# A gated mix of a long convolution and a routed feed-forward layer: down weights in a second set of buffers, wider transpositions, small steps on other engines, a new written order

## The chip, the core and the metric

The kernel runs on one core of a Trainium2 chip. The core has TensorE (PE), VectorE (DVE), ScalarE (ACT), GpSimd (POOL) and SyncE (SP), which here issues nearly all transfers. The metric is device time in microseconds (us) of one execution, lower is better.

## What is computed

Inputs are 2048 tokens of 512 channels, all fp32. Cut to its core:

```python
def reference(q, k, v, shift_k, ssm_k, ssm_D, w_r, w_gate, w_up, w_down, gate_w):
    g = sigmoid((q * gate_w).sum(-1, keepdims=True))
    kv = short_conv(k, shift_k) * v             # 4 causal taps per channel
    y = long_conv(kv, ssm_k) + kv * ssm_D       # 2048 taps per channel, by FFT
    a = q * y
    r = q @ w_r                                 # router: a score per token
    idx = argsort(-r)[:2]                       # the two best tokens
    x = q[idx]
    f = (silu(x @ w_gate) * (x @ w_up)) @ w_down * sigmoid(r[idx])
    b = q with f added at rows idx
    return g * a + (1 - g) * b
```

## The kernel before

The 512 channels are four groups c of 128. For each group the long convolution is a Fourier transform in two factors, 64 x 32. The step names are those of the written order:

- *taps c.x* (L166 to L179): a quarter of the short convolution. ACT multiplies by the first tap (L170). The other three are on DVE, each one instruction (L174), where TAPS has "D", or are an ACT multiply into one of two `tap` buffers (L177) and a POOL add (L179) where it has "A". Quarters 0 and 1 read one loaded kT tile, 2 and 3 the next.
- *T* (L190, L194): PE transposes two quarters; DVE multiplies by v, giving kv.
- *D* (L143): POOL adds the skip weights `drow` into rows 0 and 64 of a loaded filter tile hN. *A* (L161) transforms the filter, *C* (L206) transforms kv; an exchange by 32x32 transpositions on DVE (L152) follows each.
- *S u* (L219, L224, L231), u = 0 to 7: second factor on PE, then ACT copies half of the product, and DVE makes the complex products y. After each pair of u, two sums of 512 columns join them (L239), by SUMS on POOL ("G"), on DVE ("V"), or not at all ("E"): then PE takes more products in I.
- *I* (L259, L267, L269): inverse second factor and eviction, by EVICT on ACT or DVE. *X* (L276): DVE transposes f in place, after both I. *J* (L295 to L314): inverse first factor, gate and residual on ACT (L309) and POOL (L312), store. For the last group gate and residual are prepared by *Q* (L284, L287) and finished on DVE and POOL (L301, L304).

*G* is one step of the routed layer: the router's products on q (L341), two searches for the largest score (L328 to L365), an indirect DMA that gathers two rows (L375), gate and up products (L409), down products (L426), and an update (L434, L436). *Z0* (L439) adds the update to the stored output by an indirect DMA, which comes behind all stores.

*L* steps load: Lh (hN, 2 buffers), Lk (kT, 2), Lv (v, 3), Lq (q, 4), Lw (the tiles of q transposed, then gate, up and down weights, all in `wff`, 2 buffers), L0 to L11 constants. All loads and stores stand in one queue on SP; one that waits for its buffer holds those behind it.

The text ORDER names the steps. Each name advances its generator to its next `yield`, and each engine runs its instructions in that order. Products go to PSUM tiles `p2` with three buffers, so PE runs at most three of them ahead of what reads them.

## Time and profile before

| | us |
|---|---|
| median of 3 runs (range) | 167.28 (166.28 to 170.13) |
| the profiled execution | 168.12 |
| its span | 166.3 |
| PE busy | 133.7 (80%) |
| DVE busy | 125.6 (76%) |
| POOL busy | 108.7 (65%) |
| ACT busy | 99.8 (60%) |
| DMA | 39.73 MB, mean 239 GB/s |

A span runs from the first to the last instruction. A group's row gives the line, the engine, what is written and read, the count, the busy time, the mean of one in ns, and the idle time of the engine before them with what ended it. One PE product is two records in the trace, so counts of PE rows are double those of the order.

### The profile page before, as it was taken

To read this page: it belongs to the slowest core of one execution; us is meant where nothing else is said; L and a number is where in the kernel's file an instruction comes from. 1 tells how busy PE (TensorE), PEld (TensorE's weight loads), DVE (VectorE), ACT (ScalarE), POOL (GpSimd) and SP (SyncE) were. 2 spreads that over 40 slices of the span, in tenths; PEclk is the share of its full clock that TensorE was granted. 3 is DMA by queue.
4 is the path that set the end of the run, shared out by engine and by line. 5 is a ranking of instruction groups with operands and counts; after the bars stand their busy time and mean duration, and the time that the engine had idled before them with its cause. 6 is when DMAs were issued, how large, how long until landed. Compare 5 with 4: busy or idle time off the path is not lost.

```text
span 166.3 us, 4904 instructions
## 1 busy us (share of the span) xinstructions
PE 133.7 (80%) x2036; PEld 61.3 (37%) x2036; DVE 125.6 (76%) x140; ACT 99.8 (60%) x188; POOL 108.7 (65%) x103
## 2 busy tenths in 40 slices
...
GB/s 142 265 380 312 341 341 362 302 309 222 342 417 307 8 123 353 130 73 279 195 325 324 165 200 236 240 180 286 233 221 230 128 310 147 318 262 116 234 196 1
DMA packets 16377, 39.73 MB, mean 239 GB/s; under 512 B 2264, under 2 KB 2786, under 8 KB 16228
## 3 DMA queue, kind: packets, MB, share of 16 engines
...
q14 instruction: 5, 0.04, 0.1%
HBM read 35.22 MB, written 4.20 MB: 237 GB/s over the span
## 4 chain that ended last, share of the span: by engine, by line
PE 58%; DMA 16%; DVE 14%; issue 4%; SPq 2%; POOL 2%; ACT 2%; POOLq 1%; DVEq 0%
PE p L219 11%; PE p L259 11%; PE p L206 9%; PE p L161 7%; PE ps L295 5%; DMA wff<-in_wd_dram 5%; PE pf L409 4%; DMA wrg<-in_wrg_dram 4%; DVE f L276 4%; DMA pe<-in_qrow_dram,ti 3%; PE pf L341 3%; DMA kT<-in_kT_dram 2%; PE p L295 2%; DVE e L152 2%; DVE y L231 2%
## 5 line engine op out<-in xcount | busy, mean ns | idle before, releaser
L179 POOL TENSOR_TENSOR acc<-acc,tap 128x512 f32<-128x512 f32 x36 | 46.0, 1287 | 4.7 <-ACT tap L177 2.0
L231 DVE TENSOR_TENSOR y<-p,g 128x1024 f32<-128x1024 f32 x32 | 37.6, 1213 | 9.1 <-ACT g L224 5.6
L152 DVE STREAM_TRANSPOSE e<-p 128x1024 f32<-128x1024 f32 x32 | 38.3, 1234 | 5.3 <-PE p L206 3.6
L239 POOL TENSOR_TENSOR y<-y 128x512 f32<-128x512 f32 x30 | 38.2, 1292 | 4.4 <-DVE y L231 4.3
L219 PE MATMUL p<-e,w 64*32 64x256 f32 x1024 | 34.6, 387 | 2.0 <-DVE y L231 1.6
L177 ACT ACTIVATE tap<-kT,shk 128x512 f32<-128x512 f32 x36 | 25.7, 718 | 8.7 <-POOL acc L179 8.7
L224 ACT ACTIVATE g<-p 128x512 f32<-128x512 f32 x32 | 19.2, 603 | 13.1 <-PE p L219 11.4
L309 ACT ACTIVATE acc<-ps,omg,gcol 128x128 f32<-128x128 f32 x48 | 18.1, 458 | 12.4 <-PE ps L295 12.0
L312 POOL TENSOR_TENSOR qN<-acc,qN 128x512 f32<-128x512 f32 x12 | 15.4, 1290 | 12.4 <-ACT acc L309 12.4
L219 PEld LDWEIGHTS p<-e,w 64*32 64x32 f32 x1024 | 16.9, 106 | 17.8 <-ACT f L267 3.7
L276 DVE STREAM_TRANSPOSE f<-f 128x1024 f32<-128x1024 f32 x16 | 19.1, 1226 | 0.8 <-ACT f L267 0.7
L267 ACT ACTIVATE f<-p 128x1024 f32<-128x1024 f32 x15 | 16.0, 1097 | 5.3 <-PE p L259 5.3
L259 PE MATMUL p<-y,w 32*64 32x512 f32 x272 | 19.1, 600 | 0.0
L161 PE MATMUL p<-hN,w 64*128 64x512 f32 x64 | 18.1, 656 | 0.9 <-DVE e L152 0.6
L170 ACT ACTIVATE acc<-kT,shk 128x512 f32<-128x512 f32 x16 | 11.3, 715 | 11.0 <-DMA kT<-in_kT_dram 10.4
L206 PE MATMUL p<-kv,w 64*128 64x512 f32 x64 | 17.2, 646 | 0.7 <-DVE e L152 0.5
L143 POOL TENSOR_TENSOR hN<-hN,drow 1x32 f32<-1x32 f32 x16 | 4.3, 266 | 19.5 <-DMA drow<-in_drow_dram 12.1
L190 PE MATMUL p<-ident,acc 64*128 64x64 f32 x128 | 6.5, 240 | 11.8 <-DVE acc L174 9.6
L295 PE MATMUL ps<-f,vv 128*64 128x128 f32 x192 | 13.2, 277 | 0.1
L174 DVE SCALAR_TENSOR_TENSOR acc<-kT,shk,acc 128x512 f32<-128x512 f32 x12 | 8.7, 749 | 6.1 <-ACT acc L170 5.9
L295 PEld LDWEIGHTS ps<-f,vv 128*64 128x64 f32 x192 | 10.3, 134 | 7.2 <-issue 3.7
L194 DVE TENSOR_TENSOR kv<-p,vN 128x512 f32<-128x512 f32 x16 | 10.6, 690 | 2.9 <-PE p L190 1.5
...
## 6 DMA issues: line engine op xcount, KB each, us to landing
...
```

The lines of the kernel that those rows point to most:

```text
L152: nc.vector.transpose(ee[c][:, i, b * 16:(b + 1) * 16].rearrange("p d k e -> p d e k"), p)
L161: nc.tensor.matmul(p[:, j], w1[r], hs.get(t)[r, 16 * (b % 2):16 * (b % 2) + 16], start=True, stop=True)
L177: nc.scalar.activation(s, w[j], AF.Copy, scale=shk[:, c, j:j + 1])
L179: nc.gpsimd.tensor_add(acc, acc, s)
L206: nc.tensor.matmul(p[:, par].rearrange("p (d e) m -> p d e m", e=2), w1[r], x[r], start=True, stop=True)
L219: nc.tensor.matmul(p[32 * j:32 * j + 32, b, ri].rearrange("p i d -> p (i d)"), w2[r, 4 * u + j, 32 * ri:32 * ri + 32], e[r, :, u + 8 * j, ...
L224: nc.scalar.activation(g, p[:, :, :, 0], AF.Copy)
L231: nc.vector.tensor_mul(y[:, u % 2], p[:, :, :, 1].unsqueeze(3).to_broadcast(shape), g.unsqueeze(2).to_broadcast(shape))
L239: eng.tensor_tensor(w[:, :, 0, n], w[:, :, 0, n], w[:, :, 1, 1 - n], op=op)
L259: nc.tensor.matmul(pp[kp // 2][64 * h:64 * h + 64, kp % 2], w3[r, n], y[w][r, :, v, k], start=(t == 0), stop=(t == last), skip_group_check ...
L276: nc.vector.transpose(w, w)
L295: nc.tensor.matmul(p[64 * par:64 * par + 64, i, :], vv[:, par * 16 + mb * 4 + i, :], ff[c][:, :, par * 16 + mb * 4 + i, :], start=(i == 0) ...
```

## The change

- The down weights are cut by output columns into two halves of each block. One half goes through `wff`, the other through the hN buffers, which are free after the last A. Both halves of a block are multiplied apart, 256 columns each. The tiles of q transposed are cut in the same way, so one tile now serves one G step.
- X transposes 2048 columns at once, two X in place of four.
- The skip weights are loaded as 65 rows with zeros between, by one load, and D is one POOL instruction in place of two.
- In group 0, quarters 1 and 3 of the taps go from DVE to ACT and POOL (6 of 12 instructions).
- Small steps of G go from DVE to POOL (the test for the maximum, the score update, the index) and ACT (copies, 1 - g, token index, factors, update).
- The last pair of S is summed on DVE, in place of 8 more products on PE.
- A one-column activation comes first on ACT.
- ORDER is written anew.

```diff
-TAPS = ["DDDD", "AAAA", "AAAA", "AAAA"]
-SUMS = ["GGGG", "GGGG", "GGGG", "GGGE"]
+TAPS = ["DADA", "AAAA", "AAAA", "AAAA"]
+SUMS = ["GGGG", "GGGG", "GGGG", "GGGV"]
...
-Lk L0 taps0.0 Lk L1 Lk Lw L2 Lh Lk Lv Lw L3 L8 L4 taps0.0 taps0.1 taps0.0 taps0.1 taps0.0 taps0.1 taps0.1 T0.0
...
+Lk L0 taps0.0 taps0.0 Lk Lk Lh L2 L3 Lk taps0.0 L7 Lh Lv Lv taps0.0 L1 taps0.1 taps0.2 taps0.2 Lv Lw D0 taps0.2
...
-    hs = Stream("hN", [128, 32, N2], [a["hN"][t] for t in range(2 * NC)], P["h"])
+    hs = Stream("hN", [128, 32, N2], [a["hN"][t] for t in range(2 * NC)] + [a["wd"][fb, :, 1] for fb in range(4)], P["h"])
     kst = Stream("kT", [128, 1216], [a["kT"][c, x] for c in range(NC) for x in range(2)], P["k"], [(0, 704), (704, 1216)])
     vst = Stream("vN", [128, 4, DC], [a["vN"][c, x] for c in range(NC) for x in range(4)], P["v"])
     qst = Stream("qN", [128, 4, 128], [a["qN"][c, m] for c in range(NC) for m in range(4)], P["q"])
-    side_src = [a["qT"][c, :, hf * 1024:(hf + 1) * 1024] for c in range(4) for hf in range(2)]
+    side_src = [a["qT"][c, hf] for c in range(4) for hf in range(2)]
     side_src += [a[nm][hf, kc] for nm in ("wg", "wu") for hf in range(2) for kc in range(4)]
-    side_src += [a["wd"][fb, :, hf] for fb in range(4) for hf in range(2)]
+    side_src += [a["wd"][fb, :, 0].rearrange("p a b -> p (a b)") for fb in range(4)]
     sst = Stream("wff", [128, 1024], side_src, P["wff"])
...
-    once_loads = [(shk, a["shk"]), (ident, a["ident"]), (w1, a["w1"]), (drow[0:1], a["drow"][0:1]),
-                  (drow[64:65], a["drow"][1:2]), (w2[:, 0:16], a["w2"][:, 0:16]), (w2[:, 16:32], a["w2"][:, 16:32]),
+    once_loads = [(shk, a["shk"]), (ident, a["ident"]), (w1, a["w1"]), (drow, a["drow"]),
+                  (w2[:, 0:16], a["w2"][:, 0:16]), (w2[:, 16:32], a["w2"][:, 16:32]),
...
         x = hs.get(t)
-        for j in range(2):
-            r = slice(64 * j, 64 * j + 1)
-            nc.gpsimd.tensor_add(x[r, :, 0], x[r, :, 0], drow[r, t])
+        nc.gpsimd.tensor_add(x[0:65, :, 0], x[0:65, :, 0], drow[:, t])
         mark(("d", t))
...
-        w = ff[c][:, 16 * i:16 * i + 16].rearrange("p d k e -> p d e k")
+        w = ff[c][:, 32 * i:32 * i + 32].rearrange("p d k e -> p d e k")
...
         for c in range(4):
-            qt = [sst.get(2 * c), sst.get(2 * c + 1)]
-            for j in range(4):
-                nc.tensor.matmul(prg[32 * j:32 * j + 32, :], wrg[:, c, :], qt[j // 2][:, j % 2 * 512:(j % 2 + 1) * 512],
-                                 start=(c == 0), stop=(c == 4 - 1), skip_group_check=True)
-            if c < 4 - 1:
-                yield
+            for hf in range(2):
+                if c or hf:
+                    yield
+                qt = sst.get(2 * c + hf)
+                for j in range(4):
+                    nc.tensor.matmul(prg[32 * j:32 * j + 32, hf * 256:(hf + 1) * 256], wrg[:, c, :],
+                                     qt[:, j * 256:(j + 1) * 256], start=(c == 0 and hf == 0), stop=(c == 4 - 1),
+                                     skip_group_check=True)
         rgs = small([128, 512], "pe0")
...
         rcol = small([128, 16], "rcol")
-        nc.vector.tensor_copy(rcol.rearrange("p (j b) -> p j b", j=4), pv[:, 0])
-        nc.vector.tensor_scalar(omg, gcol, -1.0, 1.0, op0=ALU.mult, op1=ALU.add)
+        nc.scalar.activation(rcol.rearrange("p (j b) -> p j b", j=4), pv[:, 0], AF.Copy)
+        nc.scalar.activation(omg, gcol, AF.Copy, scale=-1.0, bias=1.0)
         yield
         cand = small([128, 16], "cand")
         where = []
         for i in range(2):
             col = yield from top_of(rcol, "col")
-            nc.vector.scalar_tensor_tensor(cand, rcol, col, wt_rev, op0=ALU.is_equal, op1=ALU.mult)
+            nc.gpsimd.tensor_scalar(cand, rcol, col, None, op0=ALU.is_equal)
+            nc.gpsimd.tensor_mul(cand, cand, wt_rev)
             w = yield from top_of(cand, f"where{i}")
             if i == 0:
                 nc.vector.tensor_scalar(cand, wt_rev, w, -3.0e38, op0=ALU.is_equal, op1=ALU.mult)
-                nc.vector.tensor_add(rcol, rcol, cand)
+                nc.gpsimd.tensor_add(rcol, rcol, cand)
             where.append(w)
         yield
         tf = small([8, 1], "tf")
-        nc.vector.tensor_mul(tf, where[1][0:8], mask[:, 1:2])
-        nc.vector.scalar_tensor_tensor(tf, where[0][0:8], mask[:, 0:1], tf, op0=ALU.mult, op1=ALU.add)
-        nc.vector.tensor_scalar(tf, tf, -1.0, first, op0=ALU.mult, op1=ALU.add)
+        nc.scalar.activation(tf, where[1][0:8], AF.Identity, bias=first, scale=mask[:, 1:2])
+        nc.scalar.activation(tf, where[0][0:8], AF.Identity, bias=tf, scale=mask[:, 0:1])
         nc.vector.tensor_copy(ti, tf)
...
-        nc.vector.tensor_tensor(oi[:, 0:1], hv, od, op=ALU.add)
+        nc.gpsimd.tensor_tensor(oi[:, 0:1], hv, od, op=ALU.add)
...
-        nc.vector.tensor_mul(fac, fac, rs[:, 0:1])
+        nc.scalar.activation(fac, fac, AF.Copy, scale=rs[:, 0:1])
...
         for fb in range(4):
-            yield
-            wt = [sst.get(24 + 2 * fb + h).rearrange("p (k f) -> p k f", k=2) for h in range(2)]
-            for s4 in range(4):
-                nc.tensor.matmul(pd[32 * s4:32 * s4 + 32, :], hT[:FS, s4, 32 * fb:32 * fb + 32], wt[s4 // 2][:FS, s4 % 2],
-                                 start=(fb == 0), stop=(fb == 3), skip_group_check=True)
+            for hf in range(2):
+                yield
+                wt = hs.get(8 + fb).rearrange("p a b -> p (a b)") if hf else sst.get(24 + fb)
+                for s4 in range(4):
+                    nc.tensor.matmul(pd[32 * s4:32 * s4 + 32, hf * 256:(hf + 1) * 256], hT[:FS, s4, 32 * fb:32 * fb + 32],
+                                     wt[:FS, s4 * 256:(s4 + 1) * 256], start=(fb == 0 and hf == 0), stop=(fb == 3),
+                                     skip_group_check=True)
         pds = small([128, D], "pe0")
...
-        nc.vector.tensor_scalar(upd, pu, fac, None, op0=ALU.mult)
+        nc.scalar.activation(upd, pu, AF.Copy, scale=fac)
...
+    warm = small([128, 1], "m")
+    nc.gpsimd.memset(warm, 0.0)
+    nc.scalar.activation(warm, warm, AF.Copy)
...
-    r["wd"] = B_w_down.reshape(4, 4, FS, D).transpose(0, 2, 1, 3).reshape(4, FS, 2, 1024)
+    r["wd"] = B_w_down.reshape(4, 4, FS, 2, 256).transpose(0, 2, 3, 1, 4).reshape(4, FS, 2, 32, 32)
```

Three places in the order. First the start, as SP's queue has it before (hN is the filter, w_78 the first factor's matrix, wff<-in_qT a tile of q transposed):

```order
L87 DMA kT<-in_kT_dram 128x704
L124 DMA shk<-in_shk_dram 128x16
L87 DMA kT<-in_kT_dram 128x512
L124 DMA ident<-in_ident_dram 128x128
L87 DMA kT<-in_kT_dram 128x704
L89 DMA wff<-in_qT_dram 128x1024
L124 DMA w_78<-in_w_dram 128x128
L89 DMA hN<-in_hN_dram 128x1024
L87 DMA kT<-in_kT_dram 128x512
L89 DMA vN<-in_vN_dram 128x512
L89 DMA wff<-in_qT_dram 128x1024
L124 DMA drow<-in_drow_dram 1x256
```

SP's queue after, from its first load on:

```order
L86 DMA kT<-in_kT_dram 128x704
L124 DMA shk<-in_shk_dram 128x16
L86 DMA kT<-in_kT_dram 128x512
L86 DMA kT<-in_kT_dram 128x704
L88 DMA hN<-in_hN_dram 128x1024
L124 DMA w_78<-in_w_dram 128x128
L124 DMA drow<-in_drow_dram 65x256
L86 DMA kT<-in_kT_dram 128x512
L124 DMA wrg<-in_wrg_dram 128x128
L88 DMA hN<-in_hN_dram 128x1024
L88 DMA vN<-in_vN_dram 128x512 x2
```

The first filter tile, w_78 and the joined drow have moved ahead of the first tile of q transposed. The same start on PE before (T is `p<-ident,acc`, A is `p<-hN`, C is `p<-kv`):

```order
L190 MATMUL p_123<-ident,acc 128x64 x16
L341 MATMUL pf<-wff,wrg 32x512 x4
L161 MATMUL p_180<-hN,w_78 128x512 x2
L190 MATMUL p_185<-ident,acc 128x64 x16
L161 MATMUL p_202<-hN,w_78 128x512 x2
L161 MATMUL p_207<-hN,w_78 128x512 x2
L161 MATMUL p_215<-hN,w_78 128x512 x2
L206 MATMUL p_218<-kv,w_78 128x512 x2
```

PE's start after:

```order
L159 MATMUL p_140<-hN,w_78 128x512 x2
L159 MATMUL p_156<-hN,w_78 128x512 x2
L188 MATMUL p_160<-ident,acc 128x64 x16
L159 MATMUL p_180<-hN,w_78 128x512 x2
L159 MATMUL p_183<-hN,w_78 128x512 x2
L342 MATMUL pf<-wff,wrg 32x256 x4
L188 MATMUL p_214<-ident,acc 128x64 x16
L159 MATMUL p_237<-hN,w_78 128x512 x2
L204 MATMUL p_247<-kv,w_78 128x512 x2
```

A0 is first now, with T0.0 between its second and third product; the router's products come later, and in halves.

Second, PE from the last search for a maximum (`pf<-ident,m`) to the gathered rows (`pf<-wtrev,pe`), before (`p<-e` is S):

```order
L331 MATMUL pf<-ident,m 128x128
L161 MATMUL p_761<-hN,w_78 128x512 x2
L219 MATMUL p_765<-e,w_80 32x256 x16
L219 MATMUL p_790<-e,w_80 32x256 x16
L190 MATMUL p_808<-ident,acc 128x64 x16
L219 MATMUL p_834<-e,w_80 32x256 x16
L385 MATMUL pf<-wtrev,pe_754 128x32 x4
```

The same stretch of PE after:

```order
L329 MATMUL pf<-ident,m 128x128
L204 MATMUL p_873<-kv,w_78 128x512 x2
L204 MATMUL p_877<-kv,w_78 128x512 x2
L217 MATMUL p_880<-e,w_80 32x256 x16
L204 MATMUL p_901<-kv,w_78 128x512 x2
L217 MATMUL p_909<-e,w_80 32x256 x16
L217 MATMUL p_928<-e,w_80 32x256 x16
L204 MATMUL p_945<-kv,w_78 128x512 x2
L385 MATMUL pf<-wtrev,pe_866 128x32 x4
```

The four C of group 2 stand in that stretch now.

Third, the end on PE, from the last S before I3.1 (`p<-y`) on, before (`pf<-wff,pe_1692` are down products, `ps<-f,vv` a J; four J of the last group follow):

```order
L219 MATMUL p_1877<-e,w_80 32x256 x16
L426 MATMUL pf<-wff,pe_1692 32x512 x4
L295 MATMUL ps<-f,vv 64x128 x8
L259 MATMUL p_1921<-y,w_81 64x512 x4
L259 MATMUL p_1922<-y,w_81 64x512 x4
L259 MATMUL p_1921<-y,w_81 64x512 x4
L259 MATMUL p_1922<-y,w_81 64x512 x4
L259 MATMUL p_1921<-y,w_81 64x512 x2
L259 MATMUL p_1922<-y,w_81 64x512 x2
L259 MATMUL p_1921<-y,w_81 64x512 x2
L259 MATMUL p_1922<-y,w_81 64x512 x2
L426 MATMUL pf<-wff,pe_1692 32x512 x4
```

The same end on PE after, up to I3.1:

```order
L217 MATMUL p_1854<-e,w_80 32x256 x16
L409 MATMUL pf<-wff,pe_959 32x224 x4
L293 MATMUL ps<-f,vv 64x128 x8
L409 MATMUL pf<-wff,pe_959 32x224 x4
L257 MATMUL p_1914<-y,w_81 64x512 x4
L257 MATMUL p_1915<-y,w_81 64x512 x4
L257 MATMUL p_1914<-y,w_81 64x512 x4
L257 MATMUL p_1915<-y,w_81 64x512 x4
```

PE after, behind that (`pf<-wff,pe_1939` and `pf<-hN` are down products, `p<-f,vv` the last J):

```order
L427 MATMUL pf<-wff,pe_1939 32x256 x4
L427 MATMUL pf<-hN,pe_1939 32x256 x4
L427 MATMUL pf<-wff,pe_1939 32x256 x4
L427 MATMUL pf<-hN,pe_1939 32x256 x4
L293 MATMUL p_1973<-f,vv 64x128 x8
L293 MATMUL p_1988<-f,vv 64x128 x8
L293 MATMUL p_1997<-f,vv 64x128 x8
L293 MATMUL p_2055<-f,vv 64x128 x8
L427 MATMUL pf<-wff,pe_1939 32x256 x4
L427 MATMUL pf<-hN,pe_1939 32x256 x4
L427 MATMUL pf<-wff,pe_1939 32x256 x4
L427 MATMUL pf<-hN,pe_1939 32x256 x4
```

All down products stand behind I3.1 now. The same end on DVE before, from the last y on:

```order
L231 TENSOR_TENSOR y<-p_1877,g 128x1024
L269 COPY f<-p_1922 128x8x64x2
L276 STREAM_TRANSPOSE f<-f 128x16x2x32 x4
L301 TENSOR_TENSOR acc<-p_1966,acc 128x512
L301 TENSOR_TENSOR acc<-p_1979,acc 128x512
L301 TENSOR_TENSOR acc<-p_2013,acc 128x512
L301 TENSOR_TENSOR acc<-p_2036,acc 128x512
L304 TENSOR_TENSOR qN<-acc,qN 128x512
```

DVE's end after:

```order
L229 TENSOR_TENSOR y<-p_1854,g 128x1024
L237 TENSOR_TENSOR y<-y 128x4x128 x2
L414 TENSOR_TENSOR pe_979<-pe_979,pf 128x448
L267 COPY f<-p_1915 128x8x64x2
L274 STREAM_TRANSPOSE f<-f 128x32x2x32 x2
L299 TENSOR_TENSOR acc<-p_1973,acc 128x512
L299 TENSOR_TENSOR acc<-p_1988,acc 128x512
L299 TENSOR_TENSOR acc<-p_1997,acc 128x512
L299 TENSOR_TENSOR acc<-p_2055,acc 128x512
L302 TENSOR_TENSOR qN<-acc,qN 128x512
```

Two sums (`y<-y`) and a product of G stand between the last y and the copy now, and two wider transpositions behind it.

More of the change, by code (lines that the diff above doesn't have):

```diff
@@ L289, in J @@
     def J(c, mb):
-        assert seen["x", c] == 4
+        assert seen["x", c] == 2
         pool, name = (ps2, "p2") if c == NC - 1 else (ps, "ps")
@@ L462, in mixed_kernel @@
         for u in range(4):
-            for f in (A, C, J, X, taps) + ((T,) if u < 2 else ()):
+            for f in (A, C, J, taps) + ((T, X) if u < 2 else ()):
                 work[f"{f.__name__}{c}.{u}"] = f(c, u)
@@ L500, in _shape_constants @@
     wtrev[:, 0:16] = 4096 - (32 * (p % 64) + 2 * m + p // 64)
-    wtrev[:8, 16:18] = np.tile(np.eye(2), (4, 1))
+    wtrev[:8, 16:18] = -np.tile(np.eye(2), (4, 1))
     wtrev[:8, 18] = 4096 * (1 + np.arange(8) // 2)
```

48 lines of the change are left out of this document (24 added, 24 removed).

## Prediction

> **What bounds the kernel now.** I read the stages first, then the groups of instructions by line, then the early and late parts in order of time. The first table is the view of windows: the stretch in us from the span's start, its length, each engine's busy time, TensorE's granted clock, the DMA share and GB/s.
>
> ```profile
> core 0: us, PE busy (x) PEld busy (x) DVE busy (x) ACT busy (x) POOL busy (x), PEclk, DMA share, GB/s
> 5.00:14.50 9.50, 1.38 (x16) 1.01 (x16) 7.09 (x11) 2.95 (x5) 0.53 (x2) 1.00 0.97 334
> 14.50:30.00 15.50, 14.47 (x80) 4.76 (x88) 13.64 (x15) 8.36 (x13) 10.19 (x12) 1.00 0.95 335
> 30.00:66.00 36.00, 32.56 (x540) 12.82 (x525) 32.52 (x46) 25.14 (x39) 31.12 (x30) 1.00 0.74 263
> 66.00:80.00 14.00, 11.53 (x152) 5.74 (x152) 11.98 (x15) 6.35 (x12) 11.93 (x11) 0.88 0.49 165
> 80.00:146.50 66.50, 64.83 (x1170) 32.18 (x1168) 49.70 (x46) 44.93 (x89) 49.63 (x43) 1.00 0.74 236
> 146.50:166.30 19.80, 8.93 (x88) 4.75 (x88) 10.67 (x11) 10.97 (x34) 5.15 (x4) 0.97 0.49 156
> ```
>
> TensorE (PE) does next to nothing before 14.5 us. From 80 to 146.5 us it is busy for 64.8 of 66.5 us: there PE is the bound. From 30 to 80 us it loses 3.4 and 2.5 us, and the clock falls to 0.88 in one stretch. In the last 19.8 us PE is busy for 8.9: that is a chain. So the time is T, the end of the last inverse product (I3.1, 146.5 us), plus a tail of 19.8 us.
>
> The groups by line, with columns for busy us, mean ns of one and idle time before:
>
> ```profile
> L219 PE MATMUL p<-e,w 64*32 64x256 f32 x1024 | 34.6, 387 | 2.0 <-DVE y L231 1.6
> L259 PE MATMUL p<-y,w 32*64 32x512 f32 x272 | 19.1, 600 | 0.0
> L161 PE MATMUL p<-hN,w 64*128 64x512 f32 x64 | 18.1, 656 | 0.9 <-DVE e L152 0.6 <-DVE y L231 0.3
> L206 PE MATMUL p<-kv,w 64*128 64x512 f32 x64 | 17.2, 646 | 0.7 <-DVE e L152 0.5 <-PE p L219 0.2
> L426 PE MATMUL pf<-wff,pe 112*32 112x512 f32 x32 | 7.4, 604 | 5.0 <-DMA wff<-in_wd_dram 5.0
> L341 PE MATMUL pf<-wff,wrg 128*32 128x512 f32 x32 | 5.6, 718 | 3.5 <-DMA wrg<-in_wrg_dram 3.5
> L152 DVE STREAM_TRANSPOSE e<-p 128x1024 f32<-128x1024 f32 x32 | 38.3, 1234 | 5.3 <-PE p L206 3.6 <-PE p L161 1.3
> L231 DVE TENSOR_TENSOR y<-p,g 128x1024 f32<-128x1024 f32 x32 | 37.6, 1213 | 9.1 <-ACT g L224 5.6 <-POOL y L239 2.7 <-PE p L259 0.8
> L194 DVE TENSOR_TENSOR kv<-p,vN 128x512 f32<-128x512 f32 x16 | 10.6, 690 | 2.9 <-PE p L190 1.5 <-DMA vN<-in_vN_dram 1.3
> L174 DVE SCALAR_TENSOR_TENSOR acc<-kT,shk,acc 128x512 f32<-128x512 f32 x12 | 8.7, 749 | 6.1 <-ACT acc L170 5.9
> L179 POOL TENSOR_TENSOR acc<-acc,tap 128x512 f32<-128x512 f32 x36 | 46.0, 1287 | 4.7 <-ACT tap L177 2.0 <-issue 1.8
> L177 ACT ACTIVATE tap<-kT,shk 128x512 f32<-128x512 f32 x36 | 25.7, 718 | 8.7 <-POOL acc L179 8.7
> ```
>
> From them one step costs: A 18.1/16 = 1.13 us, C 17.2/16 = 1.08, S 34.6/32 = 1.08, an exchange on VectorE (DVE) 38.3/32 = 1.20, kv 10.6/16 = 0.66, a tap on DVE 8.7/12 = 0.73. A tap that leaves DVE costs 0.72 on ScalarE (ACT) and 1.29 on GpSimd (POOL).
>
> **The start.** From the timeline (start, length), the seventh load's issue first, and, last, the landing of the hN loads (min, median, max):
>
> ```profile
> 3.54 0.43 SPq L124 DMA_DIRECT2D w<-in_w_dram  x1
> 12.58 0.62 POOL L143 TENSOR_TENSOR hN<-hN,drow 1x32 f32<-1x32 f32 x2 [12.13 <-DMA drow<-in_drow_dram]
> 14.51 1.93 PE L341 MATMUL pf<-wff,wrg 128*32 128x512 f32 x8 [3.51 <-DMA wrg<-in_wrg_dram]
> 29.83 4.38 PE L219 MATMUL p<-e,w 64*32 64x256 f32 x128
> DMA to landing us min/median/max: 3.8/5.1/7.9
> ```
>
> Now the first S runs at 29.8 us. After: hN, w1 and drow are the fifth to seventh loads of SP's queue; the seventh is issued at 3.5 us before, so hN and the joined add (0.3 us) are ready at 3.5 + 5.1 + 0.3 = 8.9 us (7.6 to 11.7); with the two small loads behind hN I take 9.5. PE then has A0.0 and A0.1. Its third entry, T0.0, waits for POOL: skip add, then three tap adds that stood on DVE before, 9.8 + 3 x 1.29 = 13.7 us. What limits the first S is DVE: 6 taps 4.4 + 9 exchanges 10.8 + 4 kv 2.6 = 17.8 us, against 12 taps, 8 exchanges and 4 kv = 21.0 before. It starts at 5.9 as before (the 5.9 of L174's row) and loses about 3 us, to hN and then to those POOL adds: 26.7, three us earlier than 29.8. PE has by then one A more done (+1.1), and only one eighth of the router's products where it had half (5.6 x 3/8 = -2.1). **Start: 3.1 + 1.1 - 2.1 = -2.0 us** (0 to -4.5: hN at 11.7, or no pause on DVE).
>
> **The middle.** Small steps of the router leave DVE; the rows of the four largest and of PE's wait for the gathered rows, with the S behind it:
>
> ```profile
> L361 DVE SCALAR_TENSOR_TENSOR cand<-rcol,col,wtrev 128x16 f32<-128x16 f32 x2 | 1.0, 476 | 0.1
> L365 DVE TENSOR_TENSOR rcol<-rcol,cand 128x16 f32<-128x16 f32 x1 | 1.2, 1226 | 0.0
> L370 DVE TENSOR_TENSOR tf<-where,wtrev 8x1 f32<-8x1 f32 x1 | 1.2, 1202 | 0.0
> L355 DVE TENSOR_SCALAR omg<-gcol 128x16 f32<-128x16 f32 x1 | 0.4, 382 | 0.0
> 70.04 1.07 PE L385 MATMUL pf<-wtrev,pe 2*128 2x32 f32 x8 [1.42 <-DMA pe<-in_qrow_dram,ti]
> 73.57 1.96 PE L219 MATMUL p<-e,w 64*32 64x256 f32 x32
> ```
>
> DVE is rid of 1.0 + 1.2 + 1.2 + 0.4 = 3.8 us, while 30 to 66 us shows it as busy as PE (32.5 of 36). The price is a chain that hops: two POOL steps behind each search for a maximum, each of which may stand behind a 1.29 us add, and only kv products on DVE in between. Between the last maximum and the gathered rows PE had A, S, S, T, S and now has 4 C and 3 S: 7.5 us instead of 5.2 (the T at 0.8), so the wait of 1.42 should go. What is late next is the search itself: I allow it 1 us more idle time on PE than the 3.4 of 30 to 66 us. Of the 2.5 + 14 x 0.12 = 4.2 us lost from 66 to 80, I let 3.5 go. **Middle: +1.0 - 3.5 = -2.5 us** (+1 to -5). That S took 1.96 us where one takes 1.08: after PE's pauses the clock is down. "TensorE: Matmul & The Clock Gate" of the Trainium skill (Part 1) has the clock halved after an idle window of about 3.4 us; the trace agrees in kind, with pauses shorter than that (1.42 us). By the rule the clock's part, 14 x 0.12 = 1.7 us, would not hang on these pauses, and the term would be -0.8.
>
> **The end.** From the chain of waits in order of time, then one row of the timeline:
>
> ```profile
> 142.83 3.70 PE p L259 x48
> 146.55 1.23 DVE f L269
> 147.88 4.65 DVE f L276 x4
> 152.67 3.76 PE p L295 x64
> 159.07 2.58 DMA out_dram<-qN
> 159.14 1.05 PE L426 MATMUL pf<-wff,pe 112*32 112x512 f32 x4 [1.74 <-DMA wff<-in_wd_dram]
> ```
>
> Before T: two of the four groups of down weights (L426, half of 7.4) and their waits leave PE's queue for the pause behind I3.1, where only DVE works: **-3.5** (-2 to -3.7). I3.1 loses 16 of the 272 records, 16/272 x 19.1 = 1.1 by the group, or 1.2 as a third of its own 3.70, or 1.5 against the group's mean (3.70 less 32/272 x 19.1): **-1.5** (-1.1 to -1.5). For that, two sums stand on DVE between the last y and I3.1. No such sum is in the trace; nearest are
>
> ```profile
> L304 DVE TENSOR_TENSOR qN<-acc,qN 128x512 f32<-128x512 f32 x1 | 1.7, 1701 | 0.1
> L301 DVE TENSOR_TENSOR acc<-p,acc 128x512 f32<-128x512 f32 x4 | 2.8, 692 | 2.0 <-PE p L295 1.9
> ```
>
> which bound two at 1.4 and 3.4 us. L304 is the like form, two operands in SBUF and POOL adding beside it, so I lean to 3; a J step and two groups of up weights on PE lie beside about 1 of it: **+2.0** (+0.4 to +3.4). That is also where a page speaks against the change: "GPSIMD Engine Reference" of the Trainium skill (section 8, Key points) says that POOL shares its SBUF interfaces with VectorE and collides with DVE instructions of two SBUF inputs. The trace agrees (1701 against 692 ns; 1226 ns for 16 columns). By it the two sums would be 3.4 and the term +2.4.
>
> From T to the end: two transpositions of 2048 columns for four of 1024, 4.65 less the fixed parts of two instructions. That lies between nothing and twice L355's 0.38, since an instruction on 16 columns has little else; I take 0.3. The down weights' last row came at 159.14, 12.6 us behind T, waiting for its load. After, half of the down weights lie in the hN buffers early, and the last four half-loads go out once PE has used the first four; I put the last at T + 12, half as long (0.5), so the update is ready 1 us sooner. The stores land at 159.07 + 2.58 = 161.65, and the chain goes on from them, so the update came at about that time too; both move up, and I add 0.4 for the update's lead. **Tail: -0.3 - 0.4 = -0.7**, 19.1 us (0 to -1.2).
>
> **Sum.** T: 146.5 - 2.0 - 2.5 - 3.5 - 1.5 + 2.0 = 139.0. One us comes on top because the same ACT and POOL work stands in a shorter stretch (POOL 49.6 of 66.5 us before, plus 6 x 1.29 moved to it early): 140.0. Span 140.0 + 19.1 = 159.1; the profiled execution had 168.12 us for a span of 166.3, so 160.9 on its scale. The median shown, 167.28, is 0.8 lower; I forecast **160.6 us**, this case's own range 157.5 to 163.6, chance 0.60.
>
> **Rivals.** (1) *POOL's queue stops for hN.* The third and fourth skip adds stand in front of 4 and 8 tap adds, and POOL's next sums behind those. Their loads wait on SP behind others until PE has used the buffers.
>
> ```profile
> POOL hN L143 <- DMA hN<-in_hN_dram: 6.7, 2, 4.2
> ```
>
> Two such waits cost POOL 6.7 us before, when DVE made four T inputs alone. Twice 3.35 us at the early place moves T, sums and I0 and takes away 3.4 to 6.7: 164 to 167.3, I say 165.5. For it: DMA is 95% busy then. Against: the router's loads come later, which frees the queue. 0.17.
>
> (2) *Packed too tightly.* The order saves nothing in the middle (+1 instead of -2.5) and the DVE sums cost 3.4: 160.6 + 3.5 + 1.4 = 165.5; I say 164.8 with part of it. For it: POOL and DVE 86 to 90% busy from 30 to 66 us. 0.14.
>
> (3) *Slower: the gate and up weights land too late on PE's queue.* They are taken in pairs through two buffers, and five pairs have only some 5 to 6 us of PE work between them. The pair of down loads
>
> ```profile
> 151.74 0.85 SPq L89 DMA_DIRECT2D wff<-in_wd_dram  x2
> ```
>
> was used up to 159.14, 7.4 us after its issue. Were it so for each, PE would stop five times for some 2.2 us: +11, 171.6. To cancel the gain each stop must reach 1.4. Against: L426 alone shows such waits (5.0 us), and at the end of the kernel. 0.09, the mildest of them still within 2%.
>
> **Numbers.** About 2% is what a measurement of this kernel can tell from no change: faster lies below 163.9, slower above 170.6. Faster: nearly all of 0.60, 0.04 from each of (1) and (2), and a little below this range: 0.70. Within: 0.22. Slower: 0.08. The range reaches to the first two rivals: 157.2 to 166.5.
>
> **What would show it.** Right: A0.0 on PE near 9.5 us, the first S near 27, no wait of PE for the gathered rows and no clock below 0.95 from 60 to 80 us, I3.1 ending near 140, and a tail of 19. Wrong: A0.0 near 12; POOL idle for hN between 15 and 25 us; PE waiting for wff in the pairs; L237 on DVE at 1.7 us each with I3.1 waiting on it; down weights as the last thing awaited, later than T + 13.

## The result and the profile after

The changed kernel takes **160.1 us** (median of 4 runs, 158.76 to 160.27) beside 166.9 us for the kernel before on the same chip (median of 4): a ratio of 0.960, 95% interval 0.954 to 0.966. The forecast was 160.6 us. The profiled execution took 160.21 us with a span of 158.4. The profiled executions of the kernel before and, below, of the ones with the old order and with early down weights and moved products were among the slower ones of their kernels (168.12, 175.32 and 165.40 us), so their points carry up to some 1.2 us that the medians do not. The total is close; how it comes about is not, as the same points show:

| profiled execution, us | before | forecast | after |
|---|---|---|---|
| A0.0 on PE | 16.4 | 9.5 | 10.3 |
| first S on PE | 29.8 | 26.7 | 27.2 |
| product of the gathered rows (L385) | 70.0 | – | 71.9, with 7.3 us more work ahead of it |
| T, end of I3.1 | 146.5 | 140.0 | 135.9 |
| tail, T to the end | 19.8 | 19.1 | 22.5 |

T comes 10.6 us earlier, not 6.5, and the tail is 2.7 us longer, not 0.7 shorter. First the view of windows of the kernel after, with the prediction's columns; the last two rows are cut at T:

```profile
core 0: us, PE busy (x) PEld busy (x) DVE busy (x) ACT busy (x) POOL busy (x), PEclk, DMA share, GB/s
14.50:30.00 15.50, 14.04 (x164) 5.96 (x162) 14.61 (x16) 11.04 (x17) 15.11 (x15) 1.00 0.92 315
30.00:66.00 36.00, 31.87 (x507) 13.82 (x492) 29.97 (x41) 26.38 (x43) 34.89 (x34) 1.00 0.74 257
66.00:80.00 14.00, 13.55 (x280) 6.71 (x278) 13.56 (x12) 9.55 (x17) 12.25 (x13) 1.00 0.58 214
80.00:135.90 55.90, 54.14 (x1001) 27.61 (x997) 43.52 (x38) 39.53 (x80) 43.77 (x36) 1.00 0.77 254
135.90:158.40 22.50, 12.01 (x144) 7.88 (x140) 9.19 (x8) 12.15 (x36) 5.26 (x4) 0.80 0.73 198
```

Two shorter stretches of the tail, in the same columns:

```profile
140.00:150.00 10.00, 7.69 (x100) 6.14 (x104) 4.65 (x5) 7.44 (x26) 3.85 (x3) 0.83 1.03 264
142.53:145.94 3.41, 3.41 (x36) 3.41 (x34) 1.38 (x2) 3.41 (x13) 1.28 (x2) 0.50 1.01 216
```

From 30 to 66 us PE loses 4.1 us (3.4 before); from 66 to 80 us only 0.45, at full clock (2.5 before, at 0.88). From 80 us to T it idles 1.8 us, as before (1.7), in a stretch that is 10.6 us shorter. In the tail the DMA engines moved 22.5 us x 198 GB/s = 4.5 MB; before it was 19.8 x 156 = 3.1 MB. From 140 to 150 us their share is 1.03: they have no pause. From 142.5 to 145.9 us PE has a granted clock of 0.50.

The timeline around T and in the tail (start, length; in brackets the idle time before):

```profile
130.76 2.54 POOL L237 TENSOR_TENSOR y<-y 128x512 f32<-128x512 f32 x2
133.21 2.72 PE L257 MATMUL p<-y,w 32*64 32x512 f32 x32
133.22 1.29 DVE L237 TENSOR_TENSOR y<-y 128x512 f32<-128x512 f32 x2
137.38 4.51 DVE L274 STREAM_TRANSPOSE f<-f 128x2048 f32<-128x2048 f32 x2
140.79 0.64 PE L427 MATMUL pf<-wff,pe 112*32 112x256 f32 x8 [2.19 <-DMA wff<-in_wd_dram]
141.94 5.39 PE L293 MATMUL p<-f,vv 128*64 128x128 f32 x64
149.77 0.64 PE L427 MATMUL pf<-wff,pe 112*32 112x256 f32 x8 [1.44 <-DMA wff<-in_wd_dram]
151.07 0.64 PE L427 MATMUL pf<-hN,pe 112*32 112x256 f32 x8 [0.66 <-DMA hN<-in_wd_dram]
154.05 0.36 ACT L438 ACTIVATE pe<-pf,fac 8x128 f32<-8x128 f32 x1 [1.67 <-PE pf L436]
154.73 1.41 POOL L441 DMA_INDIRECT out_dram<-pe,oidx  x1 [6.01 <-ACT pe L438]
```

I3.1 takes 2.72 us (3.71 before), the two sums on DVE 1.29 us, while POOL, whose two sums ended at 133.30, stood idle. J3 (L293) takes 5.39 us where it took 3.76. PE waits for down weights three times, the last product stands at T + 15.1, and the scatter (Z0) waits last for the update made from it, which is ready at 154.41. The view of the chain of waits ends in another row of work, qN:

```profile
134.52 1.30 POOL qN L310
135.83 6.84 DMA out_dram<-qN
142.69 5.17 DMA qN<-in_qN_dram
150.43 0.70 DVE qN L302
151.15 2.45 DMA out_dram<-qN
```

A store of 6.84 us frees the buffer for the last qN load, which takes 5.17 more; its sum and store end at 153.60, and the scatter needs them too. Two chains of transfers run side by side in the tail, then, and end within a microsecond of each other.

### The profile page after: what moved, and what is told of

The parts are those of the page before. It is cut to its first block, busy times and chain, and to the rows that moved or that the text cites. A ratio compares the mean times of both kernels' runs of the same rounds, so it can differ in the third digit from the quotient of the medians.

```text
span 158.4 us, 4996 instructions
## 1 busy us (share of the span) xinstructions
PE 129.8 (82%) x2084; PEld 64.0 (40%) x2084; DVE 116.7 (74%) x117; ACT 105.9 (67%) x201; POOL 116.2 (73%) x108
## 4 chain that ended last, share of the span: by engine, by line
PE 36%; POOL 22%; DMA 18%; ACT 8%; issue 8%; DVE 3%; SPq 2%; POOLq 1%; ACTq 0%
POOL acc L177 12%; PE p L217 12%; PE ps L293 7%; POOL y L237 6%; DMA out_dram<-qN 6%; PE p L159 5%; DMA w<-in_w_dram 5%; PE p L204 4%; DMA drow<-in_drow_dram 4%; PE p L257 4%; DMA qN<-in_qN_dram 3%; ACT f L265 3%; PE pf L409 3%; POOL qN L310 2%; ACT tap L175 2%
## 5 line engine op out<-in xcount | busy, mean ns | idle before, releaser
L177 POOL TENSOR_TENSOR acc<-acc,tap 128x512 f32<-128x512 f32 x42 | 53.5, 1287 | 2.7 <-ACT tap L175 1.9
L229 DVE TENSOR_TENSOR y<-p,g 128x1024 f32<-128x1024 f32 x32 | 38.3, 1214 | 11.2 <-ACT g L222 5.9
L175 ACT ACTIVATE tap<-kT,shk 128x512 f32<-128x512 f32 x42 | 30.2, 724 | 10.5 <-POOL acc L177 10.2
L159 PE MATMUL p<-hN,w 64*128 64x512 f32 x64 | 19.8, 708 | 10.5 <-POOL hN L141 10.3
L222 ACT ACTIVATE g<-p 128x512 f32<-128x512 f32 x32 | 19.1, 600 | 13.5 <-PE p L217 13.4
L310 POOL TENSOR_TENSOR qN<-acc,qN 128x512 f32<-128x512 f32 x12 | 15.5, 1296 | 9.2 <-DMA qN<-in_qN_dram 3.9
L274 DVE STREAM_TRANSPOSE f<-f 128x2048 f32<-128x2048 f32 x8 | 18.2, 2298 | 0.1
L204 PE MATMUL p<-kv,w 64*128 64x512 f32 x64 | 16.7, 633 | 1.3 <-DVE kv L192 1.2
L257 PE MATMUL p<-y,w 32*64 32x512 f32 x256 | 17.2, 600 | 0.0
L293 PE MATMUL ps<-f,vv 128*64 128x128 f32 x192 | 13.2, 277 | 0.0
L159 PEld LDWEIGHTS p<-hN,w 64*128 64x128 f32 x64 | 5.8, 210 | 17.9 <-POOL hN L141 11.1
L293 PEld LDWEIGHTS ps<-f,vv 128*64 128x64 f32 x192 | 10.3, 134 | 6.0 <-issue 2.3
L192 DVE TENSOR_TENSOR kv<-p,vN 128x512 f32<-128x512 f32 x16 | 10.6, 700 | 0.4 <-PE p L188 0.3
L302 POOL TENSOR_TENSOR qN<-acc,qN 128x512 f32<-128x512 f32 x3 | 3.8, 1283 | 9.1 <-DMA wff<-in_wd_dram 8.8
L204 PEld LDWEIGHTS p<-kv,w 64*128 64x128 f32 x64 | 5.7, 184 | 10.0 <-issue 2.5
```

The lines of the kernel that those rows point to most:

```text
L159: nc.tensor.matmul(p[:, j], w1[r], hs.get(t)[r, 16 * (b % 2):16 * (b % 2) + 16], start=True, stop=True)
L175: nc.scalar.activation(s, w[j], AF.Copy, scale=shk[:, c, j:j + 1])
L177: nc.gpsimd.tensor_add(acc, acc, s)
L204: nc.tensor.matmul(p[:, par].rearrange("p (d e) m -> p d e m", e=2), w1[r], x[r], start=True, stop=True)
L222: nc.scalar.activation(g, p[:, :, :, 0], AF.Copy)
L229: nc.vector.tensor_mul(y[:, u % 2], p[:, :, :, 1].unsqueeze(3).to_broadcast(shape), g.unsqueeze(2).to_broadcast(shape))
```

## The experiments

All medians are of 4 runs (10 where VectorE has the small steps without omg, 6 for the last kernel). The kernel before, timed beside each, stayed between 166.6 and 167.5 us, so that the runs can be set against the 160.1 us of the changed kernel. Points in us of each profiled execution; single executions scatter, so where the edit lies elsewhere the first S still stands between 26.0 and 27.5 us, and from the gathered rows to T it is 63.5 to 65.6 us (changed kernel, undone taps, omg alone, filling products):

| changed kernel with | median | first S | gathered rows | T | tail |
|---|---|---|---|---|---|
| nothing else | 160.1 | 27.2 | 71.9 | 135.9 | 22.5 |
| taps of group 0 all on VectorE | 163.1 | 30.2 | 74.5 | 140.1 | 22.3 |
| router's small steps on VectorE | 168.8 | 26.7 | 80.9 | 145.3 | 22.6 |
| omg alone on VectorE | 163.8 | 26.6 | 75.7 | 139.1 | 22.5 |
| small steps on VectorE, but not omg | 165.6 | 27.5 | 76.7 | 140.9 | 22.8 |
| last two sums on TensorE | 159.8 | 26.0 | 70.7 | 135.3 | 22.5 |
| (not the changed kernel: small parts in the order of before) | 175.1 | 33.0 | 74.0 | 151.4 | 22.1 |
| down weights through wff only | 168.7 | 27.1 | 71.9 | 136.2 | 30.6 |
| filling products in PE's pause | 160.9 | 26.9 | 71.5 | 137.0 | 22.9 |
| last qN tiles in a free buffer | 160.7 | 26.9 | 71.4 | 136.2 | 22.9 |
| down weights early, products at their places | 162.8 | 26.2 | 70.9 | 138.8 | 22.8 |
| down weights early, products in the pause | 164.2 | 26.1 | 71.0 | 138.4 | 25.3 |
| both, loads at 100 us and earlier qN | 163.7 | 26.7 | 71.6 | 142.6 | 19.9 |

**The start: the taps.**

```diff
-TAPS = ["DADA", "AAAA", "AAAA", "AAAA"]
+TAPS = ["DDDD", "AAAA", "AAAA", "AAAA"]
```

> The changed kernel with the four taps of the first group all on VectorE again (six of its taps come back from ScalarE and GpSimd); all else as changed. Theory of the prediction: VectorE sets the first S. Six taps of 0.7 us are 4.2 us more on VectorE, against which it no longer waits for GpSimd's adds; the first S on TensorE moves from 27.2 us to 30 (+2 to +3.5), and the end by as much: 162 to 163.5 us. Rival: the skip rows and the hN loads set the first S, and VectorE has slack before it: first S within 0.7 us of 27.2, time within 0.8 us of 160.1. Second rival: the start moves by 3 us but later pauses of TensorE absorb it: first S near 30, time within 1 us of 160.1.

Measured: 163.09 us (ratio to before 0.978, interval 0.967 to 0.989). PE's timeline in this kernel:

```profile
30.18 3.38 PE L217 MATMUL p<-e,w 64*32 64x256 f32 x96
74.47 1.07 PE L385 MATMUL pf<-wtrev,pe 2*128 2x32 f32 x8
```

The first S is 3.0 us later, the gathered rows 2.5, the end 4.0 in the profile and 3.0 by the medians. The first theory holds: VectorE sets the first S, and nothing later takes the loss back.

**The small steps.** All the router's small steps go back to VectorE; the two that matter below:

```diff
-        nc.scalar.activation(omg, gcol, AF.Copy, scale=-1.0, bias=1.0)
+        nc.vector.tensor_scalar(omg, gcol, -1.0, 1.0, op0=ALU.mult, op1=ALU.add)
...
-            nc.gpsimd.tensor_scalar(cand, rcol, col, None, op0=ALU.is_equal)
-            nc.gpsimd.tensor_mul(cand, cand, wt_rev)
+            nc.vector.scalar_tensor_tensor(cand, rcol, col, wt_rev, op0=ALU.is_equal, op1=ALU.mult)
```

> The changed kernel with the router's small steps (the copy of the gathered column, the two tie steps, the add of the candidates, the two index steps, omg, the scale and the update) back on VectorE; the order of the work as changed. Theory of the prediction: they cost VectorE some 3.8 us between 50 and 70 us, and TensorE gets half to all of it, so 162 to 164 us, with the loss between TensorE's products for the router and the gathered rows. Rival: VectorE has as much slack there as these steps take, and a chain on one engine hops less: the gathered rows come 1 to 2 us earlier and the time is 159.5 to 160.5 us.

Measured: 168.77 us, more than either theory and more than the whole change gains; the gathered rows come 9.0 us later. The timeline of this kernel shows one instruction of 16 columns that takes 6.2 us:

```profile
56.40 4.95 POOL L177 TENSOR_TENSOR acc<-acc,tap 128x512 f32<-128x512 f32 x4
57.61 6.21 DVE L355 TENSOR_SCALAR omg<-gcol 128x16 f32<-128x16 f32 x1
61.29 2.50 POOL L237 TENSOR_TENSOR y<-y 128x512 f32<-128x512 f32 x2
65.17 0.45 PE L329 MATMUL pf<-ident,m 128*128 128x128 f32 x1 [8.28 <-DVE m L326]
70.30 0.17 DVE L365 TENSOR_TENSOR rcol<-rcol,cand 128x16 f32<-128x16 f32 x1
```

It starts while GpSimd adds, and ends at 63.82 us, 0.03 us after the last of five more adds. PE waits 8.3 us for the maximum behind it, and its granted clock is 0.50 from 60.3 to 70.5 us. L365, which took 1.23 us before, takes 0.17 here, when GpSimd's queue is empty. So the next two runs put omg alone back, and all but omg.

> The changed kernel with one instruction of 16 columns back on VectorE: omg (L355), which took 0.38 us there before the change and 6.21 us in the run with all small steps undone, where it ended 0.03 us after GpSimd's queue of adds had run dry. Theory: this one instruction needs something that GpSimd holds from add to add, so it waits until GpSimd's queue is empty; then it takes 3 us or more again and the time is 164 to 170 us, most of what all the small steps cost together. Rival: it was one of several steps, and the chain of waits on one engine made the loss; then omg takes under 1 us and the time is within 1 us of 160.1.

> The changed kernel with all the router's small steps back on VectorE except omg, which stays on ScalarE. Theory that omg's wait made the loss: 159.5 to 162 us; the two-operand steps of L361, L365 and L370 may each wait for one add of GpSimd (1.2 us, as before the change) and move the gathered rows by up to 2 us. Rival, that the other steps carry the loss: over 164 us with the gathered rows at 76 us or later instead of 72.

Measured: 163.80 us with omg alone (ratio 0.982, 0.967 to 0.998); 165.58 us with the others (0.996, 0.990 to 1.001). With omg alone:

```profile
56.04 2.50 POOL L177 TENSOR_TENSOR acc<-acc,tap 128x512 f32<-128x512 f32 x2
57.14 1.44 DVE L355 TENSOR_SCALAR omg<-gcol 128x16 f32<-128x16 f32 x1 [1.16 <-ACT gcol L352]
59.92 0.44 PE L329 MATMUL pf<-ident,m 128*128 128x128 f32 x1 [3.43 <-DVE m L326]
60.30 3.72 PE L257 MATMUL p<-y,w 32*64 32x512 f32 x32
```

With the others, omg on ScalarE:

```profile
60.10 4.13 DVE L361 SCALAR_TENSOR_TENSOR cand<-rcol,col,wtrev 128x16 f32<-128x16 f32 x1
61.68 2.52 POOL L237 TENSOR_TENSOR y<-y 128x512 f32<-128x512 f32 x2
66.85 0.24 DVE L361 SCALAR_TENSOR_TENSOR cand<-rcol,col,wtrev 128x16 f32<-128x16 f32 x1
```

Both times the slow instruction ends 0.03 to 0.04 us behind a run of GpSimd's adds (58.54 and 64.20). The mechanism of the theory holds; that it hangs on omg does not: omg took 1.44 us, not over 3, since only one more add stood in GpSimd's queue, and without omg the tie step L361 met the longer queue and waited 4.1 us instead of 0.24. What such a wait costs is more than its length. With omg alone PE's pause grew to 3.43 us, and the inverse products behind it took 3.72 us instead of 1.97 at a lower clock (0.50 from 58.7 to 65.5 us, 0.91 over 30 to 66 us). The first maximum later by 1.7 us (59.65 against 57.93 us) and these products longer by 1.75 are nearly the whole 3.7. With the others the clock is 0.50 from 59.8 to 63.2 and from 66.6 to 70.0 us; how much of that loss is the wait itself and how much the clock, these runs do not separate.

"GPSIMD Engine Reference" of the Trainium skill (section 8, Key points) names VectorE's instructions with two SBUF inputs, and those in a mode with two ports, as the ones that collide with GpSimd. L361 has two inputs, so the trace agrees; omg has one, and no run here shows in which mode it ran. That the collision lasts until GpSimd's run of adds stops, section 8 does not say; these three rows show it. It is not always so: in the kernel before, L361 took 0.72 us at 51.19 and ended 0.03 us behind one add that two more followed without a gap. What decides that, no run shows.

**The order.** The kernel before, in its own order, with the taps, the small steps, the wide transpositions, the joined skip adds and the sums changed:

```diff
-TAPS = ["DDDD", "AAAA", "AAAA", "AAAA"]
+TAPS = ["DADA", "AAAA", "AAAA", "AAAA"]
-SUMS = ["GGGG", "GGGG", "GGGG", "GGGE"]
+SUMS = ["GGGG", "GGGG", "GGGG", "GGGV"]
```

> The order of the work as before, with the small parts of the change only: half of the first taps off VectorE, the small router steps moved, transpositions of 2048 columns, joined skip adds, the last pair's sums on VectorE. Not in it: the weights loaded by columns, the down weights in the hN buffers and the new order. Theory of the prediction: of the 6.8 us gained, the taps (about 3) and the small steps (1 to 2) and 0.5 of the rest are here, 162 to 163.5 us, and the down weights' 3.5 us stay in TensorE's queue ahead of T. Rival: without the order the small parts lie in pauses, since TensorE waits then for the router's loads and the down weights: 165.5 to 167 us, no better than before. Third: the small parts are nearly all of it, under 161.5.

Measured: 175.06 us (ratio to before 1.044, 1.026 to 1.061): slower than before by over 4%, which no theory allowed. The first S comes at 33.0 us, 3.2 later than before, T 5.0 later. The view of waits of this kernel:

```profile
PE p L166 <- POOL acc L155: 3.5, 2, 3.1
POOL acc L155 <- ACT tap L153: 15.9, 7, 6.2
```

In the old order ScalarE's taps stand where GpSimd waits 15.9 us for them (2.0 before), and the T products (L166) wait 3.5 us for GpSimd, beside 7.3 for VectorE (9.6 for VectorE before). Two of the edits whose undoing costs 3 and 8.7 us in the new order are in this kernel, and it loses; which of its five edits costs how much was not separated. From 66 to 80 us PE is busy for 9.03 of 14 us. Why the tail is 22.1 us here as well, no run shows.

**The two sums.**

```diff
-SUMS = ["GGGG", "GGGG", "GGGG", "GGGV"]
+SUMS = ["GGGG", "GGGG", "GGGG", "GGGE"]
```

> The changed kernel with the last pair's two sums back on TensorE (I3.1 has 48 records instead of 32, no sum on VectorE). By the prediction's terms (-1.5 for the products, +2.0 for the sums) it would be 0.5 us faster. By the changed kernel's trace (two sums took 1.29 us on VectorE, sixteen products 1.0 to 1.5) T moves by -0.3 to +0.2. Theory that the tail is set by the down weights' loads and the stores and not by T: under 0.4 us either way. A time over 160.9 or under 159.3 speaks against all three.

Measured: 159.76 us (ratio to before 0.962, 0.952 to 0.973): no difference from the changed kernel. In the profile the gathered rows come 1.2 us earlier, before the edit has any work, so T is measured from there: 64.6 us against 64.0. I3.1 takes 3.70 us instead of 2.72 and starts 0.35 us earlier. That would be a gain of 0.6 us of T by the sums, but it is less than the scatter of this stretch (63.5 to 65.6 us): shown is only that both ways cost the same within it.

**The tail: which chain?** First the down weights through wff alone:

```diff
-                wt = hs.get(8 + fb).rearrange("p a b -> p (a b)") if hf else sst.get(24 + fb)
+                wt = sst.get(24 + 2 * fb + hf)
```

> The changed kernel with the down weights through the two wff buffers alone, all eight half-loads one behind the other, none in the hN buffers; the order else as changed. Theory of the prediction: the down products wait for a landing each pair (5 to 7 us from the issue), the last one comes at 20 us or more behind T instead of 15, and the end moves by 2 to 5 us: 162 to 165 us. Rival: the stores and the qN loads set the end, and the update has that much slack: under 161 us.

Measured: 168.71 us, T as in the changed kernel, the tail 8.1 us longer. PE's last products of the update:

```profile
157.47 2.30 PE L427 MATMUL pf<-wff,pe 112*32 112x256 f32 x16 [4.87 <-DMA wff<-in_wd_dram]
```

The mechanism holds at nearly twice the size: the last down products came at T + 21, not T + 15, and the end follows them. So in this order the hN buffers are worth more than the whole gain: without them it is no faster than the kernel before (167.3 us beside it).

Then PE's clock. Three products that nobody reads go into the pause behind I3.1:

```diff
+    def fill(n):
+        for _ in range(n):
+            p = ps.tile([128, 4, DC], F32, name="ps")
+            nc.tensor.matmul(p.rearrange("p a b -> p (a b)"), ident, w2.rearrange("p a b -> p (a b)")[:, 0:512],
+                             start=True, stop=True)
+        yield
```

> The changed kernel with three products of 512 columns, whose results nobody reads, in TensorE's pause behind the last inverse product, so that its pauses there are shorter than 1.2 us. Theory of the clock: J3 takes 3.8 to 4.3 us instead of 5.4 at a granted clock near 1, and the time falls by 1 to 1.6 us, to 158.5 to 159.1. Theory of the loads: J3 gets shorter, but the last down weights and the last qN load land when they did, and the time is within 0.5 us of 160.1.

```profile
143.00 3.83 PE L293 MATMUL p<-f,vv 128*64 128x128 f32 x64
150.82 0.64 PE L427 MATMUL pf<-wff,pe 112*32 112x256 f32 x8 [2.61 <-DMA wff<-in_wd_dram]
```

J3 takes 3.83 us instead of 5.39, and the time is 160.88 us: no gain. PE only waits longer for the weights. J3 was slow, but not on the path.

Then the qN chain: the last group's four tiles go into the exchange buffer that is free by then, so no load waits for a store.

```diff
+        if c == NC - 1:
+            return spare(512 * mb, 512).rearrange("p (m d) -> p m d", m=4)
+        return qst.get(4 * c + mb)
```

> The changed kernel with the last group's four qN tiles in the exchange buffer that is free by then, so that their loads wait for no store; places in the order as changed. In the changed kernel the last qN load was issued at 142.7 us, when a store that had been issued at 135.8 landed, and the last pair of down weights stood behind it on SyncE's queue until 143.6. Theory that this chain sets the end: the last qN load is issued near 136, the last down weights near 142, the last sums follow J3 directly, and the time falls by 1 to 2.5 us, to 157.6 to 159.1. Rival, that the transfers themselves fill the DMA until the end (share 1.03 from 140 to 150 us): the loads are issued earlier and land when they did, time within 0.6 us of 160.1.

```profile
139.35 0.42 SPq L154 DMA_DIRECT2D e<-in_qN_dram  x1
142.06 0.35 SPq L88 DMA_DIRECT2D hN<-in_wd_dram  x1
150.29 0.64 PE L448 MATMUL pf<-wff,pe 112*32 112x256 f32 x8 [1.87 <-DMA wff<-in_wd_dram]
151.40 0.64 PE L448 MATMUL pf<-hN,pe 112*32 112x256 f32 x8 [0.48 <-DMA hN<-in_wd_dram]
```

The last qN load is issued 3.3 us earlier and the last down weights 1.6 us earlier, and these are used when they were (151.40 against 151.07). 160.66 us: the rival holds. From 140 to 150 us the DMA share is 1.03 to 1.06 here; what is issued earlier lands hardly earlier: the last qN load at 147.72 us instead of 147.87.

Then the down weights alone: all eight half-loads into that buffer, from 106 us on, with the products at their places or moved into the pause.

```diff
+    def fetch_wd():
+        for k in range(8):
+            if not wde:
+                wde.append(epool.tile([128, 2, DC // 2, 32, 2], F32, name="e").rearrange("p i d k e -> p (i d k e)"))
+            nc.sync.dma_start(wde[0][:FS, 1024 * k:1024 * k + 1024], a["wd"][k // 2, :, k % 2].rearrange("p a b -> p (a b)"))
+            yield
```

> The changed kernel with all eight half-loads of the down weights put into the second exchange buffer, which is free after the third column group, from about 100 us on, and twelve of the sixteen groups of down products in the pause behind the last inverse product. Theory: in the changed kernel the end waits for the late down weights and the last qN load, both in a DMA that is full from 140 to 150 us (share 1.03), and TensorE's pause before the last sums lowers its clock (J3 at 5.4 us instead of 3.8). Then the tail after the last inverse product falls from 22.5 us to 19 to 20.5 and the time to 157 to 158.6 us. Rival: the two stores and the qN loads behind them on SyncE's queue set the tail; then the update is ready early, the stores land as before, and the time is 159.5 to 160.5 us. Third: the early loads collide with the gate and up weights and T moves up by 1 us or more: over 160.5.

> As the run with the early loads of the down weights, but the down products stay at the places of the changed kernel: four groups in the pause, twelve... the rest behind the last sums' first pieces. It tells the loads from the clock. If the loads alone count: within 0.5 us of the run with the products moved. If TensorE's empty pause and its lower clock count: J3 still takes 5 us or more, and the time is 1 to 2 us above that run.

Measured: 164.20 us with the products moved and 162.81 with them at their places, in both the third theory: T comes 2.4 and 2.9 us later. Of the second run's own two theories neither came: it is 1.4 us faster than the first, though its J3 takes 5.15 us. With the products at their places the tail is 22.8 us, no shorter, because now the qN chain is last: the chain of waits of that kernel has

```profile
140.35 6.66 DMA out_dram<-qN
154.47 2.23 DMA out_dram<-qN
```

and between the two the last qN load, ACT's Q steps and the sum. So each of the two chains covers the other: taking away one leaves the tail at 22.8 or 22.9, although with the early down weights it moves only 22.8 us x 146 GB/s = 3.3 MB. With the products moved the tail is even 25.3 us; in its chain a qN load takes 8.16 us to land.

Last, both taken away: four of the down half-loads about 100 us and the last qN tiles in the free buffer, two of them issued together, the products in the pause, the sums on TensorE.

In the order four tokens "Le" stand between "S2.5 Lw" and "J0.0 J0.0" of the third column group. In the code:

```diff
-        for fb in range(4):
+        for fb in (2, 3, 0, 1):
...
+                if fb >= 2:
+                    wt = spare(2048 + 1024 * (2 * fb + hf - 4), 1024)
```

> The changed kernel with the transfers of the tail spread over earlier stretches: half of the down weights (the third and fourth quarter) loaded at about 97 us into the exchange buffer that is free by then, where the DMA share is 0.59 from 100 to 110 us; the last group's qN tiles there too, the first two of them issued together; all down products in TensorE's pause behind the last inverse product; the last pair's sums on TensorE. Theory: the tail of 22.5 us is set by what the DMA has to move from 131 us on (share 1.0 from 140 to 150), of which 1.8 MB go; J3 runs at 4 to 4.5 us because the pause is filled, the last sum is ready at 148, the stores land at 150.5, and the time is 156 to 158 us. Rival: the early loads push the gate and up weights and the qN loads back, as in the runs with the early loads of all eight halves (T up by 2.4 to 2.9 us), and GpSimd's sums with them: then the tail shrinks to 20 but T moves to 138, and the time is 159.5 us or more.

Measured: 163.67 us (ratio to before 0.981, 0.972 to 0.989). The tail is 19.9 us, 2.5 shorter, with 19.9 us x 113 GB/s = 2.3 MB, and J3 takes 3.74 us: as the theory said. But T comes 6.6 us later, far more than the rival allowed, and the time is on the rival's side (159.5 us or more). SyncE's queue and POOL in this kernel:

```profile
102.72 2.31 SPq L466 DMA_DIRECT2D e<-in_wd_dram  x4
108.38 0.66 SPq L88 DMA_DIRECT2D wff<-in_wu_dram  x1
119.25 0.97 PE L430 MATMUL pf<-wff,pe 128*32 128x224 f32 x8 [2.85 <-DMA wff<-in_wu_dram]
120.78 1.27 POOL L331 TENSOR_TENSOR qN<-acc,qN 128x512 f32<-128x512 f32 x1 [11.63 <-DMA qN<-in_qN_dram]
```

The four loads were to go at 97 us, but stood waiting for their buffer (an S on PE still to read it) until 102.7, and everything behind them on SyncE's queue moved: an up weight's load issued at 108.4 landed 10.8 us later, a qN load was issued at 114.8 instead of 105.7, and POOL, waiting 11.6 us for it, held its sums back. No kernel tried here is faster than the changed one by more than the runs scatter.

## Why the prediction came out right

By the sum it was right; by its steps it was right in the first half and wrong twice behind, in opposite directions: T came 4.1 us earlier than forecast and the tail is 3.4 us longer. That the total is off by only 0.5 us is luck. (The sum itself, 160.9 less 0.8, gives 160.1 on the median's scale; why I wrote 160.6, the prediction does not say.)

- **Start, -2.0, and middle, +1.0 - 3.5: right in size.** The gathered rows come 1.9 us later with 7.3 us more work ahead of them (an A, four C, a T and an S by the rows of before): 5.4 us are gained up to there. PE's idle time gives 3.9 of it: 2.5 up to the first S (14.2 us before, 11.7 after), which comes 2.6 us earlier (forecast 3.1); 0.7 lost from there to 66 us (forecast 1.0); 2.1 from 66 us to the rows (2.2 before, 0.1 after). The other 1.5 are products that took less time, 0.9 of them the router's (5.6 to 4.7 us). The clock's part of the -3.5 lies behind the rows: from 70 to 80 us its mean was 0.83 before, a loss of 1.7 us, and is 1.00 after. With the taps undone, the first S loses these 3 us again.
- **What the small steps are worth: wrong reason.** I counted their 3.8 us on VectorE. The runs show that their length is not it: in the new order, omg or L361 on VectorE waits for GpSimd's fuller queue, and that costs 3.7 us (omg), 5.5 (the others) or 8.7 (all). These are not gains over the kernel before, where omg took 0.38 us and L365 1.23. I had L365's 1226 ns for 16 columns and read it as one collision with a price, not as a wait for the other queue.
- **Down weights out of PE's queue, -3.5, and I3.1, -1.5: right in kind.** Half of 7.4 us is 3.7; I3.1 is 1.0 us shorter, by the group's mean 1.1; I took 1.5 from a mixed reading of the same rows.
- **Two sums, +2.0, and tightness, +1.0: the steps that failed ahead of T.** The sums took 1.29 us, the lower bound (1.4), because POOL had finished its own two sums and stood still; I leaned to the upper bound for a POOL add that the new order does not have there. What they cost on the path is within the scatter (0.35 us in one pair of executions). And PE idles as little from 80 us to T as before (1.8 against 1.7 us), so nothing came on top. Behind the gathered rows T gained 5.1 us (76.4 - 64.0 - 7.3), where these four terms gave 2.0 and the clock 1.7. With nothing on top, 0.35 for the sums and 1.0 for I3.1 they give 5.9, as near as that stretch's scatter allows.
- **Tail, -0.7: the step that failed behind T.** I moved the down products behind T, put "the last at T + 12", and left out what else the DMA engines move there. It came at T + 15.1. Six of the eight half-loads (448 KB each) are issued from 131.8 us on, 4.1 us ahead of T, where before four were issued from 142.0 on, 4.5 us ahead of a later T. Two more half-loads are 0.9 MB, and the tail moves 1.4 MB more; with the qN loads and stores the DMA engines are full from 140 to 150 us. The tail is 2.7 us longer instead of 0.7 shorter. The filling products show that it is not the clock, and the early qN tiles that issuing earlier does not help, which leaves the transfers themselves. That less to move makes the tail shorter is not shown alone: with 3.3 MB it was 22.8 us, held by the qN chain, and the last kernel (2.3 MB, 19.9 us) also has its qN tiles early, its pause filled and T 6.6 us later.
- **The rivals.** None of the three came: POOL's wait for hN falls ahead of the first skip add only (10.3 us of PE, at the start), PE never waits for gate and up weights in the changed kernel. The third had its mechanism right for this queue, though: it appears as soon as four loads are put in front of the up weights.
- **The signs named.** A0.0 at 10.3 us was between "right" and "wrong"; drow's landing released it, and the first S came 0.5 us later than forecast. The sign "later than T + 13" for the down weights came true, and the time held only because T was 4 us better than forecast.
